# Turning normed tiles with VectorE and scratch memory instead of TensorE, and rebuilding the first weight's sums one group later

## The chip, the cores and the metric

The kernel runs on one core of a Trainium2 chip. The metric is the time of one execution on the device, in microseconds (us), and less is better. The engines are TensorE (PE; its weight loads are listed as PEld), VectorE (DVE), ScalarE (ACT), GpSimd (POOL) and SyncE (SP), which in this kernel issues nearly all DMAs. Each engine runs its own instructions in program order and waits at an instruction until what it needs is ready.

## What is computed

Inputs are q, k and v of shape (8, 8, 576, 64), and two weights of shapes (512, 2048) and (2048, 512), all float32.

```
for each batch, head and chunk of 64 rows:                 # chunk attention
    out = softmax(q_c @ k_c.T / 8) @ v_c
x = out as (8, 576, 512)                                   # heads side by side
u = x + real(fft(fft(x, axis=1), axis=2))                  # Fourier mix
un = (u - mean(u)) / sqrt(var(u) + 1e-6)                   # per row of 512
result = u + relu(un @ w_ch1) @ w_ch2                      # (8, 576, 512)
```

## The kernel before

**Tiles and groups.** The 8 x 576 rows are cut into tiles of 128 rows. Each of the first eight groups holds the four tiles of one batch (two "low", two "high"); the ninth group holds the four tiles of rows left over. For each group the two big products are made: the *up* product (512 to 2048 columns, `w_ch1`) and the *down* product (2048 to 512, `w_ch2`). I write U0 to U8 and D0 to D8 for these phases; they alternate on PE: U0, D0, U1, D1 and so on.

**Two forms of the products.** `up_plain` and `down_plain` use the weights as they are: 64 matmuls of 128x128 by 128x512 a phase. `up_halves` and `down_halves` cut each matrix into halves and make seven half-sized products instead of eight (112 matmuls of 128x128 by 128x256 a phase). They need sums and differences of the weights' quarters. `keep1` (for `w_ch1`) and `keep2` (for `w_ch2`) make these sums once and write the seven operands to scratch memory `s1` and `s2`; from then on `fetch(1)` reads 256 KB slabs of `s1` into ten places in `wa`, and `fetch(2)` reads 1 MB slabs of `s2` into three places in `wb`, over the plain weights. `first_of = {1: 1, 2: 1}` says from which group on the halved forms are used: here both from group 1 on. They need sums of activations too: `combined(g, q_)` (line 860, four VectorE operations) makes them from the turned tiles, for one low and one high tile; `q_` is 0 or 1.

**Turning.** The up product wants the normed rows with the 512 columns on the partitions. `normed(g, s)` (line 830) makes a normed tile `un`; `turned(g, s)` (line 848) transposes it by four 128x128 PE transposes (`turn`, line 329/333) into PSUM, and copies it to `unT` with ACT (line 858) or DVE (line 856).

**Order of the work.** All order is written by hand. `mlp(g)` yields after each step: 16 steps `t` in an up phase and in `down_plain`, 14 steps (`k` = 0 to 13; product `o = k // 2`, low or high tiles `r = k % 2`) in `down_halves`. After each step the launching loop (lines 1213 to 1248) issues a share of the next batch's attention and Fourier work, the rounding of weight pieces at the start, and the steps of `conv1` (`keep1`) and `conv2` (`keep2`). In `down_halves(g)` the next group's tiles are normed at k = 3, 5, 7, 9, turned in the middle of the matmuls of k = 5, 7, 9, 11 (line 1088), and combined at k = 9 and 11 (line 1116). Finished output tiles are stored at k = 10 to 13 by `store` (line 871): a low tile by one 256 KB DMA (line 876), a high tile by two of 128 KB (line 885). Slabs are fetched at the end of odd k (line 1131, issue at line 933).

**The step in question at the start.** `conv1` runs in D0 from t = 23 on, three steps of VectorE work at a time, and from t = 29 the first ten slabs of `s1` are fetched. `conv2` runs on VectorE in U1, four steps at a time, while U1 already uses slabs of `s1`.

Of the kernel before, what the change touches and what calls it, by code (L numbers as in the profile page):

```python
# [8 lines left out]
FP32 = mybir.dt.float32  # L9
# [7 lines left out]
def kernel(  # L17
# [32 lines left out]
    nc = tc.nc  # L50
    B, H, S, D = q.shape
    DM = H * D
# [7 lines left out]
    KD = DM // 128  # L60
# [39 lines left out]
    UP = (1, 0, 2, 3, 4, 6, 5)  # L100
    s1 = dram.tile([HF // 2, NO, 128, 2 * 2 * 128], FP32, name="s1")
    s2 = dram.tile([NO, 128, HF * HM], FP32, name="s2")
    NS1, NS2, Z1, Z2 = 10, 3, 2 * 2 * 128, HF * HM
    slab1 = [wa[:, i * Z1:(i + 1) * Z1].rearrange("p (k r f) -> p k r f", r=2, k=2) for i in range(NS1)]
    slab2 = [wb[:, i * Z2:(i + 1) * Z2].rearrange("p (m e) -> p m e", m=HF) for i in range(NS2)]
# [742 lines left out]
    def turned(g, s):  # L848
# [8 lines left out]
        else:  # L857
            nc.scalar.copy(unT[:, :, s * 128:(s + 1) * 128], pt)

    def combined(g, q_):  # L860

        unT = unTs[g]
        cl, ch = slice(q_ * 128, (q_ + 1) * 128), slice(256 + q_ * 128, 256 + (q_ + 1) * 128)
        b11, b12, b21, b22 = unT[:, 0:2, cl], unT[:, 0:2, ch], unT[:, 2:4, cl], unT[:, 2:4, ch]
        t1, t2, t4 = (tt[:, o, :, cl] for o in range(3))
        nc.vector.tensor_tensor(out=t1, in0=b12, in1=b11, op=ALU.subtract)
        nc.vector.tensor_tensor(out=t2, in0=b22, in1=t1, op=ALU.subtract)
        nc.vector.tensor_tensor(out=b12, in0=b22, in1=b12, op=ALU.subtract)
        nc.vector.tensor_tensor(out=t4, in0=b21, in1=t2, op=ALU.subtract)
# [18 lines left out]
    def keep1(i):  # L888

        f, kk = divmod(i, 2)  # L890
        lo, hi = slice(f * 512, (f + 1) * 512), slice(DFF // 2 + f * 512, DFF // 2 + (f + 1) * 512)
        a11, a12, a21, a22 = w1[:, kk, lo], w1[:, 2 + kk, lo], w1[:, kk, hi], w1[:, 2 + kk, hi]
        late = [xall[:, r, 0:DM] for r in (NR + 2, NR + 3, 2 * G + 2, 2 * G + 3)]
        o1, o2, o3, o4 = late if i % 2 else (yall[:, j] for j in range(4))
        for out_, in0, in1, op in (
            (o1, a21, a22, ALU.add), (o2, o1, a11, ALU.subtract),
            (o3, a11, a21, ALU.subtract), (o4, a12, o2, ALU.subtract),
        ):
            nc.vector.tensor_tensor(out=out_, in0=in0, in1=in1, op=op)
            yield  # L900
        to = s1.rearrange("a o p (k x) -> p a o k x", k=2)[:, 2 * f:2 * f + 2]
        for o, a in enumerate((a11, o2, o1, o3, a12, o4, a22)):
            nc.sync.dma_start(out=to[:, :, o, kk], in_=a.rearrange("p (a x) -> p a x", a=2))
        yield

    def keep2(i):

        m = 2 * i
        b11, b12 = w2[:, m:m + 2, 0:HM], w2[:, m:m + 2, HM:DM]
        b21, b22 = w2[:, HF + m:HF + m + 2, 0:HM], w2[:, HF + m:HF + m + 2, HM:DM]  # L910
        to = xall[:, 0:4, 0:DM] if i % 2 else yall
        o1, o2, o3, o4 = (to[:, j].rearrange("p (m e) -> p m e", m=2) for j in range(4))
        for out_, in0, in1, op in (
            (o1, b12, b11, ALU.subtract), (o2, b22, o1, ALU.subtract),
            (o3, b22, b12, ALU.subtract), (o4, b21, o2, ALU.subtract),
        ):
            nc.vector.tensor_tensor(out=out_, in0=in0, in1=in1, op=op)
            yield
        to = s2.rearrange("o p (m e) -> o p m e", m=HF)
        for o, a in enumerate((b11, o2, o1, o3, b21, b22, o4)):  # L920
            nc.sync.dma_start(out=to[o, :, m:m + 2], in_=a)
        yield

    first_of = {1: 1, 2: 1}
    n_slab = {1: 0, 2: 0}

    def fetch(which):
# [140 lines left out]
    def down_halves(g, h1):  # L1068
        pas, pbs = {}, {}
        for o in range(NO):  # L1070
            w = slab2[((g - first_of[2]) * NO + o) % NS2]
            for r in range(2):
                cl, ch = slice(r * 128, (r + 1) * 128), slice(256 + r * 128, 256 + (r + 1) * 128)
                low, high = groups[g][r], groups[g][2 + r]
                olow, ohigh = os_[:, 2 * r], os_[:, 2 * r + 1]
                a, b = tmp[:, r, 0], tmp[:, r, 1]
                if o == 0:
                    pas[r] = ps_f.tile([128, 2, 256], FP32, tag="ff", name="pa")
                if o == 2:
                    pbs[r] = ps_f.tile([128, 2, 256], FP32, tag="ff", name="pb")  # L1080
                dst = (pas, pas, pbs, pbs, pas, pbs, pbs)[o][r][:, (0, 1, 0, 1, 0, 0, 1)[o]]
                lhs = (
                    h1[:, 0:HF, cl], ys[:, :, cl], xs[:, :, cl], h1[:, 0:HF, ch],
                    h1[:, HF:KF, cl], ys[:, :, cl], h1[:, HF:KF, ch],
                )[o]
                k = 2 * o + r
                for m in range(HF):
                    if m == HF // 2 and g + 1 < NG and k in range(5, 5 + 2 * G, 2):
                        turned(g + 1, (k - 5) // 2)
                    nc.tensor.matmul(  # L1090
                        out=dst, lhsT=lhs[:, m], rhs=w[:, m],
                        start=(o in (0, 2) and m == 0), stop=(m == HF - 1), skip_group_check=True,
                    )
                if o == 0:
                    nc.scalar.copy(a, dst)
                elif o == 1:
                    nc.vector.tensor_tensor(out=b, in0=dst, in1=a, op=ALU.add)
                elif o == 2:
                    nc.vector.tensor_tensor(out=a, in0=dst, in1=b, op=ALU.add)
                elif o == 3:  # L1100
                    nc.vector.tensor_tensor(out=ohigh[:, HM:DM], in0=dst, in1=ohigh[:, HM:DM], op=ALU.add)
                    nc.gpsimd.tensor_tensor(out=olow[:, HM:DM], in0=b, in1=natural(low)[:, HM:DM], op=ALU.add)
                    nc.gpsimd.tensor_tensor(out=ohigh[:, 0:HM], in0=b, in1=natural(high)[:, 0:HM], op=ALU.add)
                elif o == 4:
                    nc.vector.tensor_tensor(out=olow[:, 0:HM], in0=dst, in1=natural(low)[:, 0:HM], op=ALU.add)
                elif o == 5:
                    nc.vector.tensor_tensor(out=olow[:, HM:DM], in0=dst, in1=olow[:, HM:DM], op=ALU.add)
                    store(low, olow)
                else:
                    nc.vector.tensor_tensor(out=ohigh[:, 0:HM], in0=dst, in1=ohigh[:, 0:HM], op=ALU.add)  # L1110
                    store(high, ohigh)
                if g + 1 < NG:
                    for j in range(G):
                        if k == 3 + 2 * j:
                            normed(g + 1, j)
                        if k == 5 + 2 * j and j >= 2:
                            combined(g + 1, j - 2)
                if r == 1:
                    if o == 1:
                        for j in range(0, HF, 2):  # L1120
                            two = ys[:, j:j + 2]
                            nc.gpsimd.tensor_tensor(
                                out=two, in0=h1[:, HF + j:HF + j + 2, lo], in1=two, op=ALU.subtract
                            )
                    if o == 2:
                        for i in range(2):
                            nc.gpsimd.tensor_tensor(
                                out=os_[:, 2 * i + 1, HM:DM], in0=tmp[:, i, 0],
                                in1=natural(groups[g][2 + i])[:, HM:DM], op=ALU.add,
                            )  # L1130
                    fetch(2)
                yield
# [7 lines left out]
    with tc.manual_schedule():  # L1140
# [59 lines left out]
        for g in range(NG):  # L1200
            begin.append(begin[-1] + (KF if g < first_of[1] else 2 * HF) + (KF if g < first_of[2] else 2 * NO))
        ready_at = [begin[g] + (2 * KF - 7 if g < first_of[2] else 2 * HF + 4) for g in range(NG)]
        conv2 = iter([step for i in (2, 3, 0, 1) for step in [keep2(i)]])
        conv1 = iter([step for i in range(4) for step in [keep1(i)]])

        def chain(gens):
# [6 lines left out]
        for g in range(NG):  # L1213
            for _ in mlp(g):
# [15 lines left out]
                    if t <= 2 or t < KF and t % 4 == 0 or t >= KF + 3:  # L1230
                        round_next()

                if n_w > len(pieces) and KF + 7 <= t < begin[1] - 3:
                    for _ in range(3):
                        next(conv1, None)
                if t == begin[1] - 3:
                    for _ in conv1:
                        pass
                    for _ in range(NS1):
                        fetch(1)  # L1240
                if begin[1] <= t:
                    for _ in range(4):
                        next(conv2, None)
                if t == begin[1] + KF // 2 + 2:
                    for _ in conv2:
                        pass
                    for _ in range(NS2):
                        fetch(2)


# [47 lines left out]
```

## Time and profile before

| what | value |
|---|---|
| median of 3 runs | 1115.32 us (1114.74 to 1116.82) |
| the profiled execution | 1116.82 us |
| its span, first to last instruction | 1115.0 us, 1.8 us less than its time |
| PE busy | 1069.9 us, 96% of the span |
| DVE, ACT, POOL busy | 601.9, 304.7, 259.4 us |
| DMA, queue of SP | 149652 packets, 197.54 MB, 60.2% of 16 engines |

Phases on PE, by the first matmul of each:

| phase | from | to | length | its own matmuls |
|---|---|---|---|---|
| D0 | 115.53 | 193.96 | 78.43 | 59.22 (plain, 128x512) |
| U1 | 193.96 | 278.52 | 84.56 | 55.2 (halved) |
| D1 | 278.52 | 340.87 | 62.35 | 50.8 |
| U2 | 340.87 | 399.76 | 58.89 | 50.2 |
| D2 | 399.76 | 456.63 | 56.87 | 50.4 |
| D3, D4, D5 | | | 61.52, 56.87, 61.52 | 50.5 each |
| D6 | 861.20 | 914.71 | 53.51 | 49.8 |
| D7 | 963.06 | 1013.16 | 50.10 | 49.2 |
| U8 | 1013.16 | 1061.51 | 48.35 | 48.35 |
| D8 | 1061.51 | 1110.02 | 48.51 | 48.5 |

How to read it: each matmul of float32 stands as two records. A phase's length less its own matmuls is other PE work (attention, Fourier, turning) and idle time. D8 has no next group to turn, and U8 and D8 have nothing beside their products.

### The profile page before, as it was taken

What the parts mean: (1) busy time and instruction counts of PE and PEld (TensorE: products, weight loads), DVE (VectorE), ACT (ScalarE), POOL (GpSimd) and SP (SyncE); (2) the same over time, 40 slices, a digit from 0 to 9 for tenths busy, and PEclk for the clock granted to TensorE, in tenths of its full rate; (3) what the DMA queues carried; (4) which work ended last, traced back from release to release, by engine and by line L of the source; (5) the groups of instructions that cost most, each with busy time, mean ns of one, the idle gap of its engine ahead of it and who ended that gap; (6) DMA issues with size and microseconds to landing.
All of it is one profiled execution on the core that took longest, in us unless ns stands there. A gap on an engine that the chain in (4) does not pass through costs nothing.

```text
span 1115.0 us, 19182 instructions
## 1 busy us (share of the span) xinstructions
PE 1069.9 (96%) x7114; PEld 869.0 (78%) x7114; DVE 601.9 (54%) x1322; ACT 304.7 (27%) x746; POOL 259.4 (23%) x387
## 2 busy tenths in 40 slices
PE   8999999488999999999999999999999999999998
PEld 6645444366888888888888888888888888888887
DVE  4899988465355645573556356644554434323521
ACT  4787453022112231232122211322133102201210
POOL 4201000005311523051405140334033401130130
PEclk9999999789999999999999999999999999999999
DMA  8778548798756845785467547773754346446332
GB/s 165 227 209 192 145 147 258 223 308 242 221 163 196 215 135 187 212 219 157 162 189 203 176 152 203 190 210 130 205 193 114 114 156 198 138 151 198 85 114 76
DMA packets 152005, 200.11 MB, mean 179 GB/s; under 512 B 66574, under 2 KB 104462, under 8 KB 144744
## 3 DMA queue, kind: packets, MB, share of 16 engines
q1 hardware_dynamic: 149652, 197.54, 60.2%
q8 instruction: 57, 0.93, 0.4%
q0 software_dynamic: 512, 0.68, 0.3%
q10 hardware_dynamic: 1748, 0.66, 0.2%
q14 instruction: 36, 0.29, 0.1%
HBM read 174.56 MB, written 24.12 MB: 178 GB/s over the span
## 4 chain that ended last, share of the span: by engine, by line
PE 84%; DMA 5%; DVE 5%; ACT 3%; SPq 2%; issue 1%; POOL 1%; DVEq 0%; ACTq 0%; POOLq 0%
PE pb L1090 20%; PE pa L1041 19%; PE pa L1090 15%; PE pb L1041 14%; PE pt L333 3%; PE dn L995 3%; PE up L954 2%; PE mix L700 2%; PE more_z L652 2%; DMA wa<-s 2%; PE sc L384 1%; PE xp L432 1%; PE z L652 1%; DMA xall<-in_moe_w_ch_dram 1%; DMA k<-in_k_dram 1%
## 5 line engine op out<-in xcount | busy, mean ns | idle before, releaser
L1041 PE MATMUL pa<-unT,wa 128*128 128x256 f32 x768 | 184.0, 383 | 3.3 <-DVE h L1057 2.7
L1041 PEld LDWEIGHTS pa<-unT,wa 128*128 128x128 f32 x768 | 145.6, 191 | 24.2 <-DVE h L1057 3.5
L1041 PE MATMUL pb<-wa 128*128 128x256 f32 x512 | 124.7, 387 | 5.1 <-DMA wa<-s 3.3
L942 POOL TENSOR_TENSOR h<-h 128x256 f32<-128x256 f32 x64 | 55.7, 874 | 317.3 <-PE pb L1041 150.5
L1090 PE MATMUL pa<-wb,h 128*128 128x256 f32 x512 | 115.6, 380 | 0.0
L1090 PE MATMUL pb<-wb,h 128*128 128x256 f32 x512 | 114.9, 379 | 0.0
L1041 PEld LDWEIGHTS pb<-wa 128*128 128x128 f32 x512 | 97.8, 193 | 20.4 <-issue 3.7
L1090 PEld LDWEIGHTS pa<-wb,h 128*128 128x128 f32 x512 | 96.1, 190 | 13.0
L1090 PEld LDWEIGHTS pb<-wb,h 128*128 128x128 f32 x512 | 96.3, 190 | 12.6
L1047 DVE TENSOR_TENSOR wa<-pb,wa 128x256 f32<-128x256 f32 x64 | 27.0, 425 | 69.3 <-ACT wa L1046 69.1
L1041 PE MATMUL pa<-wa 128*128 128x256 f32 x256 | 61.3, 382 | 1.0 <-DMA wa<-s 1.0
L1046 ACT COPY wa<-pa 128x256 f32<-128x256 f32 x64 | 23.8, 373 | 137.2 <-PE pa L1041 130.6
L1041 PE MATMUL pb<-unT,wa 128*128 128x256 f32 x256 | 60.6, 379 | 0.1
L995 PE MATMUL dn<-wb,h 128*128 128x512 f32 x128 | 59.2, 612 | 1.2 <-ACT h L965 1.2
L1090 PE MATMUL pb<-wb,yall 128*128 128x256 f32 x256 | 58.2, 381 | 0.0
L1090 PE MATMUL pa<-wb,yall 128*128 128x256 f32 x256 | 57.9, 380 | 0.0
L1061 ACT ACTIVATE h<-h 128x512 f32<-128x512 f32 x64 | 39.7, 628 | 66.4 <-DVE h L1060 66.2
L1090 PE MATMUL pb<-wb 128*128 128x256 f32 x256 | 57.7, 379 | 0.0
L1055 ACT ACTIVATE h<-pa 128x256 f32<-128x256 f32 x64 | 24.6, 384 | 112.5 <-PE pa L1041 112.3
L1041 PEld LDWEIGHTS pb<-unT,wa 128*128 128x128 f32 x256 | 48.6, 190 | 7.1 <-DVE wa L1049 0.5
L1041 PEld LDWEIGHTS pa<-wa 128*128 128x128 f32 x256 | 47.9, 190 | 7.8 <-issue 1.1
L1090 PEld LDWEIGHTS pa<-wb,yall 128*128 128x128 f32 x256 | 47.7, 190 | 6.4
(247 smaller groups left out, 1633.0 us busy)
## 6 DMA issues: line engine op xcount, KB each, us to landing
wa<-s SPq DMA_DIRECT2D x224, 256.0 KB
wb<-s SPq DMA_DIRECT2D x56, 1024.0 KB
xall<-in_moe_w_ch_dram SPq DMA_DIRECT2D x22, 512.0 KB
q<-in_q_dram SPq DMA_DIRECT2D x96, 112.0 KB
k<-in_k_dram SPq DMA_DIRECT2D x96, 112.0 KB
v<-in_v_dram SPq DMA_DIRECT2D x124, 64.0 KB
yall<-in_moe_w_ch_dram SPq DMA_DIRECT2D x10, 512.0 KB
s<-yall SPq DMA_DIRECT2D x16, 256.0 KB
```

The costliest lines, as they stand in the source:

```text
L333: nc.tensor.transpose(pt[:, j, :], src(j), ident)
L652: nc.tensor.matmul(out=out_, lhsT=lhsT[p], rhs=tk[p, i, T // 2 if T != 5 else 0, cols], start=start, stop=stop, skip_group_check=True,)
L700: nc.tensor.matmul(out=mix[:, cols], lhsT=zt[:, T], rhs=tab, start=(T == 0), stop=(T == 3), skip_group_check=True,)
L942: nc.gpsimd.tensor_tensor(out=h1[:, m, hi], in0=h1[:, m, lo], in1=h1[:, m, hi], op=ALU.subtract)
L954: nc.tensor.matmul(out=up, lhsT=w1[:, kk, m * 128:(m + 1) * 128], rhs=unT[:, kk], start=(kk == 0), stop=(kk == KD - 1), skip_group_check=True,
L995: nc.tensor.matmul(out=dn, lhsT=h1[:, m, s * 128:(s + 1) * 128], rhs=w2[:, m, :], start=(m == 0), stop=(m == KF - 1),)
L1041: nc.tensor.matmul(out=dst, lhsT=w[:, kk, r], rhs=rhs[o][:, kk], start=(o in (0, 1) and kk == 0), stop=(kk == 1), skip_group_check=True,)
L1046: nc.scalar.copy(a, dst)
L1047: nc.vector.tensor_tensor(out=b, in0=pbs[r][:, 0], in1=a, op=ALU.add)
L1055: nc.scalar.activation(out=h1[:, m, lo], in_=dst, func=ACTF.Relu)
L1061: nc.scalar.activation(out=h1[:, HF + m], in_=h1[:, HF + m], func=ACTF.Relu)
L1090: nc.tensor.matmul(out=dst, lhsT=lhs[:, m], rhs=w[:, m], start=(o in (0, 2) and m == 0), stop=(m == HF - 1), skip_group_check=True,)
```

## The change

Three edits are made at once.

1. **Turning.** In `down_halves` the PE transposes go. After `normed(g+1, j)` at k = 3 + 2j, `flipped` transposes the tile's 32x32 blocks on VectorE into `blocks`; at k = 4 + 2j `sent` writes the blocks to scratch memory by four DMAs in pieces of 128 bytes, such that memory holds the turned tile; at k = 5 + 2j `fetched` reads 256 KB back into `unT`. `combined` moves to k = 11 (q_ = 0) and 12 (q_ = 1). This holds for groups 2 to 8; group 1 is turned by PE in `down_plain(0)` as before.
2. **First use of the halves.** `first_of[1]` goes from 1 to 2: U1 uses `up_plain`, and group 1 is not combined.
3. **Sums of weights.** `conv2` is now in D0 (VectorE, three steps at a time from t = 23), in the order 0, 1, 2, 3 and with `xall[2G:2G+4]` in place of `xall[0:4]`; `conv1` is now in U1 on GpSimd, three steps at a time in its first eight steps, with `os_` in place of rows of `xall`. The first slabs of `s2` are fetched in the middle of U1, those of `s1` at its end.

```diff
+    un_d = [dram.tile([128, KD, G * 128], FP32, name=f"un_d{i}") for i in range(2)]
...
+    def flipped(g, s):
+        if s >= len(groups[g]):
+            return
+        un = uns.pop((g, s))
+        t = three_p.tile([128, KF, 32], FP32, tag="o", name="blocks")
+        nc.vector.transpose(out=t, in_=un.rearrange("p (b f) -> p b f", f=32))
+        blocks[g, s] = t
+
+    def sent(g, s):
+        if s >= len(groups[g]):
+            return
+        t = blocks.pop((g, s))
+        to = un_d[g % 2].rearrange("(a f) k t -> f k a t", a=4)
+        for i in range(4):
+            nc.sync.dma_start(
+                out=to[:, :, :, s * 128 + 32 * i:s * 128 + 32 * (i + 1)],
+                in_=t[32 * i:32 * (i + 1)].rearrange("f (k a) t -> f k a t", a=4),
+            )
+
+    def fetched(g, s):
+        if s >= len(groups[g]):
+            return
+        if s == 0:
+            unTs[g] = one_p.tile([128, KD, G * 128], FP32, tag="unT", name="unT")
+        cols = slice(s * 128, (s + 1) * 128)
+        nc.sync.dma_start(out=unTs[g][:, :, cols], in_=un_d[g % 2][:, :, cols])
...
-        late = [xall[:, r, 0:DM] for r in (NR + 2, NR + 3, 2 * G + 2, 2 * G + 3)]
-        o1, o2, o3, o4 = late if i % 2 else (yall[:, j] for j in range(4))
+        o1, o2, o3, o4 = ((os_ if i % 2 else yall)[:, j] for j in range(4))
...
-            nc.vector.tensor_tensor(out=out_, in0=in0, in1=in1, op=op)
+            nc.gpsimd.tensor_tensor(out=out_, in0=in0, in1=in1, op=op)
...
-        to = xall[:, 0:4, 0:DM] if i % 2 else yall
+        to = xall[:, 2 * G:2 * G + 4, 0:DM] if i % 2 else yall
...
-    first_of = {1: 1, 2: 1}
+    first_of = {1: 2, 2: 1}
...
-                    if m == HF // 2 and g + 1 < NG and k in range(5, 5 + 2 * G, 2):
-                        turned(g + 1, (k - 5) // 2)
...
-                        if k == 5 + 2 * j and j >= 2:
+                            flipped(g + 1, j)
+                        if k == 4 + 2 * j:
+                            sent(g + 1, j)
+                        if k == 5 + 2 * j:
+                            fetched(g + 1, j)
+                        if k == 6 + 2 * j + (j == 2) and j >= 2:
                             combined(g + 1, j - 2)
...
-        conv2 = iter([step for i in (2, 3, 0, 1) for step in [keep2(i)]])
+        conv2 = iter([step for i in range(HF // 2) for step in [keep2(i)]])
...
-                if n_w > len(pieces) and KF + 7 <= t < begin[1] - 3:
+                if n_w > len(pieces) and t >= KF + 7:
+                    for _ in range(3):
+                        next(conv2, None)
+                if t == begin[1] - 1:
+                    for _ in conv2:
+                        pass
+                if begin[1] <= t < begin[1] + KF // 2:
                     for _ in range(3):
                         next(conv1, None)
-                if t == begin[1] - 3:
-                    for _ in conv1:
-                        pass
+                if t == begin[1] + KF // 2:
+                    for _ in range(NS2):
+                        fetch(2)
+                if t == begin[1] + KF:
                     for _ in range(NS1):
                         fetch(1)
-                if begin[1] <= t:
-                    for _ in range(4):
-                        next(conv2, None)
-                if t == begin[1] + KF // 2 + 2:
-                    for _ in conv2:
-                        pass
-                    for _ in range(NS2):
-                        fetch(2)
```

More of the change, by code (lines that the diff above doesn't have):

```diff
@@ L858, in turned @@
             nc.scalar.copy(unT[:, :, s * 128:(s + 1) * 128], pt)
+    blocks = {}
+    def flipped(g, s):
[22 more added lines that the diff above has]
+        nc.sync.dma_start(out=unTs[g][:, :, cols], in_=un_d[g % 2][:, :, cols])
     def combined(g, q_):
```

## The prediction

> **What bounds the kernel now.** I read the page's busy rows first, then the windows of single phases, the waits inside U1, and SP's own timeline at a phase boundary.
>
> ```profile
> span 1115.0 us, 19182 instructions
> ...
> PE 1069.9 (96%) x7114; PEld 869.0 (78%) x7114; DVE 601.9 (54%) x1322; ACT 304.7 (27%) x746; POOL 259.4 (23%) x387
> ...
> PEclk9999999789999999999999999999999999999999
> ```
>
> PE is busy for 96% of the span, so a change pays only by taking work off PE or by closing one of its few gaps. PE's largest hole lies in slices 8 and 9, which are U1, where PEclk also drops. The windows give, for U1, U2, D7 and D8: length, busy time (and instructions) of PE, PEld, DVE, ACT, POOL, then the granted clock, the DMA share and GB/s.
>
> ```profile
> 193.96:278.52 84.56, 60.67 (x464) 50.44 (x465) 45.88 (x102) 17.11 (x38) 17.38 (x33) 0.86 0.88 259
> 340.87:399.76 58.89, 58.49 (x415) 49.12 (x409) 35.07 (x79) 17.18 (x42) 19.95 (x34) 1.00 0.74 207
> 963.06:1013.16 50.10, 50.10 (x241) 44.12 (x240) 13.73 (x30) 2.62 (x6) 11.43 (x12) 1.00 0.42 145
> 1061.51:1110.02 48.51, 48.51 (x225) 42.37 (x223) 7.14 (x16) 1.45 (x4) 11.04 (x12) 1.00 0.30 104
> ```
>
> U2, D7 and D8 are full of PE work; U1 has 84.56 - 60.67 = 23.9 us without any, and its clock is 0.86 where the others have 1.00. The waits in U1 (who waited <- for whom: us, times, longest) say why:
>
> ```profile
> PE pt L333 <- ACT ex L410: 16.9, 1, 16.9
> ...
> DVE yall L917 <- DMA s<-yall: 15.7, 1, 15.7
> ```
>
> VectorE stands 15.7 us in `conv2`, whose buffer is still being written to scratch memory; the attention behind it is late, and PE with it.
>
> **Part 1: PE without the turning.** In D7 the turning is this, with the copy after it:
>
> ```profile
> 1004.09 0.60 PE L333 MATMUL pt<-ident,un 128*128 128x128 f32 x4
> 1004.73 0.69 DVE L856 COPY unT<-pt 128x512 f32<-128x512 f32 x1 [1.67 <-PE pt L333]
> ```
>
> D7 and D8 have the same product and differ by the turning of four tiles: 50.10 - 48.51 = 1.59 us a group, less than the 4 x 0.60 of busy time because PE's records overlap. Seven groups (2 to 8) give -7 x 1.59 = -11.1 (to -16.8 by busy time). The copy of a tile goes too (0.69 us on VectorE or 0.58 on ACT).
>
> What VectorE gets for it stands in the trace as the same form:
>
> ```profile
> L352 DVE STREAM_TRANSPOSE kT<-k 128x512 f32<-128x512 f32 x27 | 30.0, 1111 | 8.4 <-DMA k<-in_k_dram 8.2
> ```
>
> So 28 tiles x 1.11 = 31 us of VectorE, less about 14 copies x 0.69 = 10. VectorE is busy 13.73 of 50.10 us in D7 and 35 of 59 in U2, so I cost this at nothing; if that cover went, (31 - 10) / 7 = 3 us a group would show.
>
> **Part 1: the path of the last tile.** This decides the sum. Before, a tile was turned within 2 us; now it goes out (4 DMAs, 512 pieces of 128 bytes each) and back (256 KB), and PE's next up phase cannot start before `combined` has had tile 3. Its writes are issued at k = 10, on SP directly after the store of the first low output tile (line 876). SP's timeline at the end of D7 shows that store at 1003.09, the last PE work of D7 ending at 1013.16, 10.07 later:
>
> ```profile
> 1003.09 0.56 SPq L876 DMA_DIRECT2D out_dram<-wb  x1
> 1006.98 1.13 SPq L885 DMA_DIRECT2D out_dram<-wb  x2
> 1008.20 0.54 SPq L933 DMA_DIRECT2D wb<-s  x1
> 1010.36 0.55 SPq L876 DMA_DIRECT2D out_dram<-wb  x1
> ```
>
> No view prints when a DMA landed; I counted it from the semaphore updates in the trace. The L876 store lands 7.80 to 7.91 us after its issue in each of D1 to D7 and its updates come from only 2 of 16 engines, while the two halves of a high tile (L885), issued 3.9 us after it, land only 0.3 to 0.4 us after it (1010.89, then 1011.22). So what is issued behind this store has its share on the two busy engines wait, and the new writes stand just there. Steps from that store's issue: it lands at 7.85; the writes' share on those engines, 4 x 512 / 16 = 128 pieces, follows; then about 0.3 for the reading DMA, which waits for the writes; then 2.5 to 2.6 for 256 KB (a slab of `wa` lands in 2.5 at best). A piece of 128 bytes takes 11 to 12 ns on an engine in this trace (224 packets, other DMAs), one of 256 bytes 18 to 21, one of 1024 bytes 46 to 49. Those are not scattered writes. I take 16 ns, between the first two: 128 x 0.016 = 2.05, so the tile is back X = 7.85 + 2.05 + 0.3 + 2.6 = 12.8 us after the store. Bounds: 11 ns (nearest row; X = 12.2) and 49 ns (an eight times larger piece; X = 17.0).
>
> The Trainium skill, "DMA: Bandwidth & Descriptors", section "Specifications", speaks against these writes: pieces under 512 bytes do not reach line rate and are paid as read-modify-write. The small packets above do not show that, and no run here has scattered 128-byte writes; paid like whole 512-byte pieces (about 30 ns, between the rows above), an estimate by that page's rule, they would add 1.8 us to each of seven groups, and the sum would be some 12 us higher.
>
> What waits: a second `combined` is 4 operations of 0.42 on VectorE, some 1.75; PE's first matmuls of the up phase use the first sums 0.95 after tile 3 is there. Before, the up phase began 11.70 us after the store in D1 to D5 and 10.07 in D6 and D7; without the last turning (0.44 in the chain) that is 11.26 and 9.63. In D1, D3 and D5 an attention product stands ahead on PE at 10.7, and the VectorE transposes that it needs are now behind all of the second `combined` (1.75 + 1.1, less what overlaps: 2.75). Stalls:
> - D1, D3, D5: 12.8 + 2.75 - 10.7 = 4.85 each, 14.6
> - D2, D4: 12.8 + 0.95 - 11.26 = 2.5 each, 5.0
> - D6, D7: 12.8 + 0.95 - 9.63 = 4.1 each, 8.2
>
> Together 27.8; with X = 12.2 it is 23.6, with X = 17.0 it is 57. Slabs and stores queued on SP behind the waiting read of 256 KB come some 3 us later; slabs are issued about a phase before use, so I cost that at nothing, or up to 1 us a group (7) without that cover.
>
> **The clock after a stall.** In U1, after PE idle of some 3.5 us or more, the granted clock stands at 0.50 for pieces of 3.41 us (231.21 to 234.62, 258.52 to 261.93): each costs 1.7 us. About half of the five long stalls should get one: +4 (0 to 8.5). The Trainium skill, "TensorE: Matmul & The Clock Gate", Part 1, has the clock halve after an idle window of this length, in agreement.
>
> **Part 2 and 3: U1 and D0.** U1 becomes plain. D0's plain product gives its size:
>
> ```profile
> L995 PE MATMUL dn<-wb,h 128*128 128x512 f32 x128 | 59.2, 612 | 1.2 <-ACT h L965 1.2
> ```
>
> 59.2 us of matmuls, 4 more than the 55.2 that the halved form takes in U1. The other PE work of U1 is 60.67 - 55.2 = 5.5 in the window's busy time and 7.2 as a sum of its groups, so U1 has at least 64.7 to do; I take 59.2 + 7.2 = 66.4. What is late next is SP: 76 DMAs are issued from 190 on at about 0.69 us each (SP's rate in U1), with the writes of `s1`, the stores and the shift of batch 2 among them, so the last q and k tiles of that batch are turned near 241 and 248, by my count some 6 us after PE could use them. So U1 is 66.4 + 6 = 72, and 84.56 - 72 = -12.5 (-18 without that wait, -4 if the attention is as late by 8 us more). The sums of `w_ch1` move to GpSimd: 16 operations of 1.39 (line 1122 has the form: 1391 ns) are 22 us in U1, where POOL is busy 17 of 84; nothing on PE waits for them before U2. `conv2` in D0 takes the VectorE place that `conv1` had (the same 16 operations). The `combined` of group 1, which stood ahead of the last output rows of D0, goes: -1.4.
>
> **Sum.** -11.1 (turning) - 12.5 (U1) - 1.4 (D0) + 27.8 (starts of seven up phases) + 4 (clock) = +6.8. The profiled execution took 1116.82 (span 1115.0 and 1.8 around it), which is 1.5 above the median 1115.32; against the median the forecast is **1122 us**. Measurements of this kernel can tell about 0.2%, 2.2 us, from no change.
>
> **The rivals.**
> - *The forecast*: waits at the starts of U2 to U8 eat both gains. For it: a store that lands late in every group, directly ahead of the writes. Bounds: 1122 - 4 - 4 = 1114 (11 ns, no clock pieces), 1108 if U1 also gains 18; upwards 9 (26 ns a piece: 10 ns x 128 x 7), 4.5 (all clock pieces), 8.5 (U1 gains only 4) and 2 (slabs), 1146. Chance **0.55**, of which 0.05 is faster and 0.07 within 0.2%.
> - *The exchange is hidden*, the side not slower: pieces go round the two busy engines, or the queue takes DMAs side by side, so X is near 9 (1.4 for the writes beside the store, and issue, wait, and 2.6). Stalls are then about 3 and the clock keeps 1.00: 1115.3 - 25 + 3 = 1093. It wins once X is below some 9.6, the point from which U7 and U8 start on time. Against it: L885 landing just after L876 in all pairs I looked at. Chance **0.22**.
> - *Small writes are dear*: at 49 ns X = 17, stalls 57, clock +8.5: 1115.3 - 25 + 57 + 8.5 = 1156, and SP's queue falls back in every group. For it: no scattered write of 128 bytes is in this trace to say otherwise. Chance **0.13**.
> - *U1 keeps its hole*: the attention in U1 is as late as before, now behind SP's queue; nothing is gained there, so 1122 + 12 = 1134. Chance **0.10**, of which 0.03 falls within 0.2% with an exchange half hidden.
> - That the turning does not leave PE: excluded, since in `down_halves` nothing else calls it.
>
> **Numbers.** Slower by over 0.2%: (0.55 - 0.05 - 0.07) + 0.13 + 0.07 = 0.63. Faster: 0.22 + 0.05 = 0.27. Same: 0.07 + 0.03 = 0.10. The range is 1093 to 1146: it leaves out half of the hidden case (0.11) and most of the dear one (0.09), together 0.2. The forecast's own range is 1108 to 1146.
>
> **What would show it.** In the profile after: no PE work on line 333 past D0, D7 near 48.5; PE waiting at the first matmuls of U2 to U8 for VectorE's `combined`, and that for a DMA into `unT`, some 2.5 us in U3 and U5, 4 to 5 in U2, U4, U6, U7 and U8; PEclk dips there; U1 near 72 with PE waiting for q or k. If U7 and U8 start as before, the store does not hold the writes and the forecast is wrong by 25 us; if D0 to U1 grows, the SP queue there was mis-sized.

## The result, and the profile after

| | before | after |
|---|---|---|
| median of the runs beside each other | 1115.03 us (1113.09 to 1116.82) | 1139.68 us (1139.17 to 1141.52) |
| ratio, 95% interval | | 1.0224 (1.0204 to 1.0245) |
| span of the profiled execution | 1115.0 us | 1137.6 us |
| PE idle after 115 us (start of D0) | 31.0 us | 47.4 us |
| PE's time lost to a clock of 0.50 | 6.5 us | 19.3 us |

The change makes the kernel slower by 2.24% (24.65 us between the medians); 1122 was forecast. The two lower rows are counted from the trace's records of the profiled execution: the time up to PE's last instruction in which no PE instruction ran, and half of PE's busy time that lay in stretches granted 0.50.

The changed kernel's page, its busy row and its clock row:

```profile
PE 1075.8 (95%) x6906; PEld 848.9 (75%) x6906; DVE 591.8 (52%) x1272; ACT 292.6 (26%) x716; POOL 280.1 (25%) x403
...
PEclk9999999999989998999899998999899989998999
```

The one dip of before (U1) is gone. In its place stand seven, one for each group turned by scratch memory. PE's busy time is larger although it has 208 instructions less: matmuls in stretches granted 0.50 last longer and count as busy (19.3 us of PE's time against 6.5, the last row of the table).

The windows of U1, U2, D7, U8 and D8 of the changed kernel, with the columns of the prediction's windows:

```profile
191.82:253.99 62.17, 61.65 (x369) 29.31 (x368) 19.00 (x42) 12.44 (x22) 27.28 (x36) 1.00 0.73 222
321.99:381.18 59.19, 59.19 (x413) 50.27 (x409) 34.83 (x77) 17.41 (x42) 19.91 (x34) 0.97 0.74 205
978.79:1032.92 54.13, 48.51 (x226) 42.38 (x224) 14.65 (x31) 1.44 (x4) 11.43 (x12) 0.99 0.56 165
1032.92:1084.11 51.19, 51.19 (x225) 44.63 (x226) 22.38 (x54) 13.72 (x31) 5.38 (x6) 0.95 0.43 133
1084.11:1132.61 48.50, 48.50 (x225) 42.37 (x223) 7.15 (x16) 1.44 (x4) 11.04 (x12) 1.00 0.31 104
```

U1 is 62.17 us where it was 84.56, and full of work. D7's PE work is 48.51, exactly D8's, so the turning is off PE as meant; but D7 lasts 54.13, with 5.6 idle at its end, and U8 after it has a mean clock of 0.95 and takes 51.19 instead of 48.35. Up to the start of D1 the changed kernel gains 24.5 us (253.99 against 278.52); from there to the end of U8 it loses 47.1 (830.12 against 782.99).

PE's two largest waits in the whole changed kernel (who waits <- for whom: us, times, longest):

```profile
PE pb L1070 <- DVE wa L897: 23.4, 4, 6.5
PE sc L385 <- DVE kT L353: 20.1, 3, 7.3
```

The four are the starts of U3, U5, U7 and U8, which wait for `combined` (line 897). The three are attention products just ahead of U2, U4 and U6, whose VectorE transposes (line 353) stand behind `combined`. Together 43.5 us. The chain of waits from D7 into U8 tells what `combined` waited for (start, us, what):

```profile
1017.05 0.44 DVE wb L1134
...
1017.50 0.58 SPq L906
...
1018.13 0.60 SPq L877
...
1018.77 2.99 SPq L877
...
1021.80 2.42 SPq L877
...
1024.26 4.52 DMA un_d<-blocks
...
1028.92 3.03 DMA unT<-un_d
...
1031.98 0.44 DVE wa L896
...
1032.44 0.43 DVE wa L897
...
1032.92 1.22 PE pb L1070 x2
```

The store of the low tile (now line 906) is issued, then the four writes, of which the last lands at 1028.78; then the read of 256 KB, then `combined`, then PE. The second and third writes take SP 2.99 and 2.42 us to issue. By the semaphore updates the store lands at 1027.25, 9.75 after its issue, and the last write 1.53 behind it. The slab of `wb` that is issued 1.16 us ahead of the store (1016.34) lands at 1022.08, so it stands ahead of both.

### The profile page after: what moved, and what is told of

Its sections match the earlier page's. It is cut to its first block, busy times and chain, and to the rows that moved or that the text cites. A ratio compares the mean times of both kernels' runs of the same rounds, so it can differ in the third digit from the quotient of the medians.

```text
span 1137.6 us, 18806 instructions
## 1 busy us (share of the span) xinstructions
PE 1075.8 (95%) x6906; PEld 848.9 (75%) x6906; DVE 591.8 (52%) x1272; ACT 292.6 (26%) x716; POOL 280.1 (25%) x403
## 4 chain that ended last, share of the span: by engine, by line
PE 75%; DMA 10%; SPq 5%; DVE 5%; ACT 2%; issue 1%; POOL 1%; DVEq 0%; ACTq 0%; POOLq 0%
PE pa L1070 17%; PE pb L1070 14%; PE pa L1117 13%; PE pb L1117 11%; PE up L1003 4%; DMA un_d<-blocks 4%; PE up L983 3%; SPq L877 3%; PE dn L1024 3%; DMA wb<-s 3%; DMA unT<-un_d 2%; PE mix L701 2%; PE more_z L653 2%; PE sc L385 1%; PE z L653 1%; PE pt L334 1%
## 5 line engine op out<-in xcount | busy, mean ns | idle before, releaser
L1070 PE MATMUL pa<-unT,wa 128*128 128x256 f32 x672 | 163.1, 387 | 0.0
L1070 PEld LDWEIGHTS pa<-unT,wa 128*128 128x128 f32 x672 | 130.4, 196 | 19.0
L1070 PE MATMUL pb<-wa 128*128 128x256 f32 x448 | 119.0, 413 | 23.4 <-DVE wa L897 23.4
L1070 PEld LDWEIGHTS pb<-wa 128*128 128x128 f32 x448 | 91.7, 208 | 38.6 <-DVE wa L897 24.4
L1003 PE MATMUL up<-unT,wa 128*128 128x512 f32 x128 | 56.8, 595 | 0.0
L718 POOL TENSOR_TENSOR xall<-y,xall 128x513 f32<-128x513 f32 x14 | 24.0, 1711 | 124.3 <-DVE y L712 114.3
L1070 PE MATMUL pa<-wa 128*128 128x256 f32 x224 | 53.5, 382 | 0.0
L1117 PEld LDWEIGHTS pb<-wb,yall 128*128 128x128 f32 x256 | 48.2, 190 | 6.7
L1070 PE MATMUL pb<-unT,wa 128*128 128x256 f32 x224 | 52.9, 379 | 0.0
L1117 PEld LDWEIGHTS pb<-wb 128*128 128x128 f32 x256 | 48.2, 190 | 6.3
```

The costliest lines, as they stand in the source:

```text
L718: eng.tensor_tensor(out=x[:, 0:w], in0=y[:, 0:w], in1=x[:, 0:w], op=ALU.add)
L1003: nc.tensor.matmul(out=up, lhsT=w1[:, kk, m * 128:(m + 1) * 128], rhs=unT[:, kk], start=(kk == 0), stop=(kk == KD - 1),)
L1070: nc.tensor.matmul(out=dst, lhsT=w[:, kk, r], rhs=rhs[o][:, kk], start=(o in (0, 1) and kk == 0), stop=(kk == 1), skip_group_check=True,)
L1117: nc.tensor.matmul(out=dst, lhsT=lhs[:, m], rhs=w[:, m], start=(o in (0, 2) and m == 0), stop=(m == HF - 1), skip_group_check=True,)
```

## The experiments

All medians are in us; the ratio is to the kernel before, run beside it on the same chip (medians 1112.3 to 1112.7). "Idle" and "clock" are the two lower rows of the table above, each from one profiled execution, which in e2, e7 and e9 was the slowest of its runs. "New order" is the changed kernel with edits 2 and 3 alone. e2, e3, e4, e7, e11 and e13 scatter more than the others, by 6 to 14 us (e4 from 1114.3 to 1124.5), so their ratios carry the weight.

| run | what | median | ratio, 95% interval | idle | clock |
|---|---|---|---|---|---|
| e1 | new order, turned by PE | 1088.65 | 0.9789 (0.9762 to 0.9815) | 5.2 | 0 |
| e2 | before + turning by scratch memory | 1162.73 | 1.0451 (1.0411 to 1.0491) | 76.4 | 24.2 |
| e3 | after, low store on 16 engines | 1103.28 | 0.9937 (0.9909 to 0.9966) | 21.4 | 8.6 |
| e4 | after, stores behind the last read | 1120.95 | 1.0063 (1.0040 to 1.0087) | 36.7 | 8.1 |
| e7 | e3 and e4 together | 1095.86 | 0.9828 (0.9787 to 0.9870) | 18.5 | 5.0 |
| e11 | after, writes issued by ACT | 1143.55 | 1.0271 (1.0239 to 1.0303) | 52.6 | 14.0 |
| e5 | new order, three tiles by scratch memory | 1091.11 | 0.9811 (0.9797 to 0.9826) | 11.3 | 3.1 |
| e12 | e5, writes issued by ACT | 1100.87 | 0.9887 (0.9855 to 0.9918) | 17.9 | 7.5 |
| e9 | e1 + block transposes | 1092.73 | 0.9822 (0.9796 to 0.9848) | 9.3 | 1.7 |
| e10 | e9 + one plain write a tile | 1094.08 | 0.9830 (0.9806 to 0.9855) | 7.4 | 1.7 |
| e14 | e9 + four plain writes a tile | 1101.38 | 0.9889 (0.9867 to 0.9912) | 10.7 | 3.4 |
| e6 | e9 + the four writes of edit 1 | 1104.58 | 0.9939 (0.9919 to 0.9958) | 17.1 | 1.7 |
| e8 | e1, `w_ch1` sums on VectorE | 1092.22 | 0.9821 (0.9806 to 0.9835) | 8.0 | 0 |
| e13 | e1, `w_ch2` sums in U1 | 1111.04 | 0.9981 (0.9965 to 0.9997) | 19.7 | 5.7 |

### e1 and e2: the two halves of the change

e1 puts `turned` back into the matmul loop of `down_halves` and the two `combined` back to k = 9 and 11. e2 is the diff of edit 1 on the kernel before.

> The changed kernel with edits 2 and 3 only: group 1 plain, sums of w_ch2 in D0 and of w_ch1 in U1 on GpSimd; all tiles turned by PE as before. Theory (the order of the sums closes the hole in U1, 22.4 us in the trace after, and the exchange costs what D1 to U8 lost): 1115 - 25 = 1090, within 3, no idle time of PE above 2 us after U1. Rival (part of the gain before D1 came from the exchange's lighter PE, or the hole comes back later): 1097 to 1110.

> The kernel before with edit 1 only: tiles of groups 2 to 8 turned by VectorE and scratch memory, the sums' order as before. Theory: the hole of U1 stays and D1 to U8 grow by 47 us as in the trace after: 1162, within 4, seven stalls of 4.8 to 7.3 us of PE. Rival (the stalls of after come from the later sums or slabs of edits 2 and 3): below 1145.

The theory held in both. The new order alone is worth -24.0 us (1088.65 against 1112.63) and the exchange alone costs +50.1; on top of the new order the exchange costs 1139.68 - 1088.65 = +51.0 (48.6 if each is taken against its own kernel before). So the halves add up to within some 2 us and can be explained apart. e1's page shows a PE without a hole:

```profile
PE 1068.5 (98%) x7018; PEld 847.4 (78%) x7018; DVE 577.1 (53%) x1258; ACT 299.2 (28%) x730; POOL 280.6 (26%) x403
...
PEclk9999999999999999999999999999999999999999
```

e1 is also the fastest version found: 2.1% faster than the kernel before.

### e3, e4, e7: the store ahead of the writes

e3 and e4 as diffs of the changed kernel; e7 has both.

```diff
 # e3
-            nc.sync.dma_start(out=to[:, ::-1], in_=o)
+            for i in range(2):
+                nc.sync.dma_start(out=to[i], in_=o[i * CH:(i + 1) * CH])
 # e4
-                    store(low, olow)
+                    late.append((low, olow))
...
+                if k == 11:
+                    for n, o_ in late:
+                        store(n, o_)
```

> The changed kernel, with the store of a low tile cut into two DMAs of 64 rows, whose rows go out in unreversed order (this leaves out the reversal of the rows), so that it is spread over 16 engines instead of 2. Theory (the last tile's writes are held by the two engines of that store): the store lands some 5 us earlier, the tile comes back some 5 us earlier, stalls shrink from 43 us in all to under 15 and most pieces at clock 0.50 go: 1090 to 1100. Rival (many small writes, their issue and the way back are the cost themselves): above 1125.

> The changed kernel, with both output tiles of k = 10 and 11 stored on SP only after the last tile's writes and its read have been issued; every DMA keeps its form. Theory: the writes stand behind a slab of wb only, the tile is back some 5 us earlier, stalls under 15 us in all: 1085 to 1100. Rival (small writes themselves, or the slab of wb ahead of them, set the time): above 1120.

> The changed kernel with both edits: output tiles of k = 10 and 11 stored after the last read is issued, and a low tile stored by two DMAs over 16 engines with its rows unreversed (this leaves out the reversal of the rows). Theory (the two-engine store holds whatever stands behind it: the writes in the changed kernel, the slabs and loads when it is moved): neither is held now, 1080 to 1092. Rival (moving stores late costs by itself, or the small writes do): above 1100.

e3 takes back 36 of the 51 us by the medians, 32 of 48 by the ratios: less than expected (1090 to 1100) and far from the rival. Its store in D7 still lands 5.4 us after its issue; the 1 MB slab of `wb`, issued 1.1 us before it, lands only 0.35 ahead of it. Writes and read follow, and the tile is back 10.7 us after the store's issue instead of 14.45. PE's boundary waits are 18.6 us in all.

e4 failed as a remedy, in a way that tells something. Its time, 1120.95, lies at the edge of the rival's range (above 1120), but its waits are not the rival's:

```profile
PE pa L1070 <- DVE h L1086: 9.3, 3, 3.3
PE pb L1070 <- DMA wa<-s: 9.0, 6, 2.7
PE pb L1070 <- DVE wa L897: 6.0, 4, 2.2
```

The waits for `combined` fell from 23.4 to 6.0, as the theory says. But PE now waits inside the up phases, 9.0 us of it directly for slabs of `wa`. SP's own timeline shows the two low stores close behind each other:

```profile
1013.66 0.56 SPq L888 DMA_DIRECT2D unT<-un_d  x1
1014.26 0.58 SPq L906 DMA_DIRECT2D out_dram<-wb  x1
1014.95 1.18 SPq L915 DMA_DIRECT2D out_dram<-wb  x2
1016.17 1.63 SPq L962 DMA_DIRECT2D wb<-s  x1
1017.85 0.80 SPq L906 DMA_DIRECT2D out_dram<-wb  x1
```

By the semaphore updates the first lands 8.1 us after its issue, the second 13.6, and the slabs behind them 9.8 to 11.9 (the three of `wa` 11.2 to 11.9, where slabs of `wa` have a median of 4.0 in the changed kernel). So what stands behind the two-engine store on SP lands late: the writes in one order, the slabs in the other. e7, with the store on 16 engines and late, is at 1095.86: between theory (up to 1092) and rival (from 1100), still above e1. From the issue of the last tile's first write to the landing of its read, the mean of the seven groups is 13.1 us in the changed kernel, 9.0 in e3, 9.1 in e4 and 9.2 in e7. With the store spread over 16 engines, issued later, or both, this way is some 4 us shorter, and 9 us remain; how much of them is due to the slab of `wb` ahead of the writes was not tried apart. What a perfectly placed exchange could gain, the 11 us of turning, no version got.

### e11: the writes on another queue

```diff
-            nc.sync.dma_start(
+            nc.scalar.dma_start(
                 out=to[:, :, :, s * 128 + 32 * i:s * 128 + 32 * (i + 1)],
```

> The changed kernel with the four writes of a tile issued by ACT instead of SP; the read stays on SP. Theory (the writes stand behind the two-engine store because they follow it in SP's queue): they land some 5 us earlier, the tile is back some 4 us earlier, and PE's stalls fall from 43 us to 10 to 20: 1100 to 1115. Rival (the two engines themselves are busy with the store, whichever queue the writes come from): 1133 to 1142.

The time lies just past the rival's range (1143.55; the range ended at 1142), but not by the rival's mechanism: the writes hardly meet the store. In D3 ACT and SP issue as follows:

```profile
542.54 2.94 ACTq L877 DMA_DIRECT2D un_d<-blocks  x4
...
552.91 0.62 SPq L906 DMA_DIRECT2D out_dram<-wb  x1
...
554.93 0.74 SPq L888 DMA_DIRECT2D unT<-un_d  x1
```

By the semaphore updates all four writes have landed at 549.90, 11.5 us ahead of the store (561.39). From ACT the last write is issued ahead of the store in every group, by 3.5 to 9.4 us in D1 to D5 and by 0.6 and 0.25 in D6 and D7, and in D1 to D6 it lands 4.2 to 11.6 us ahead of it. So far the theory is right. But the read that brings the tile back is still on SP and is now what stands behind the store: in D3 it is issued 5.0 us after the writes have landed and takes 8.71 us, where the changed kernel's reads of the last tile take 3.03 to 3.65. In all seven groups it lands 1.4 to 3.4 us behind the store. From the end of its block transpose the last tile needs 19.3 us on average to be back, where the changed kernel needs 18.5: moving the writes alone only changed which part of its way was held. In D7 alone the writes were late too:

```profile
1016.59 2.85 ACTq L877 DMA_DIRECT2D un_d<-blocks  x4
...
1019.04 0.57 SPq L906 DMA_DIRECT2D out_dram<-wb  x1
...
1029.25 0.57 SPq L888 DMA_DIRECT2D unT<-un_d  x1
```

All four writes (the third and fourth at 1018.17 and 1018.79) are issued before the store. The first two land at once, but the third lands at 1026.24, just after a slab of `wb` that SP issued at 1018.41, and the fourth at 1029.19, 10.4 us after its issue; the store takes 12.3 us instead of 9.75. That would fit two transfers sharing the two engines, but it is one group of seven. Whether a transfer issued behind the store, such as the read, would go round it from another queue was not tried.

### e5, e12: only the last tile by PE

> The changed kernel with the fourth tile of each group turned by PE again (in the middle of k = 11, both combined at k = 11); the first three go through scratch memory. Theory (only the last tile's way back is on the path, the others have 3 us and more to spare): three quarters of the 11 us of turning are saved on the version with the new order alone, 1088.65 - 8 = 1080, within 4, no stall over 2 us at the starts of U2 to U8. Rival (the DMAs of the other tiles delay slabs and loads on SP's queue, or tile 2 is late as well): 1095 or more.

> The fourth tile turned by PE, the first three through scratch memory with their writes issued by ACT. Theory (what kept this from beating the new order alone was SP's queue): 1080 to 1087. Rival (the writes cost wherever they are issued, or ACT's work is now late): 1089 to 1095.

In e5, `flipped`, `sent` and `fetched` are called for j < 3 only, and `turned(g + 1, 3)` stands in the matmul loop of k = 11. The boundary waits are gone, and D7 is 48.79 us where e1 has 50.10. Still the total is 1091.11, no better than e1: the theory (1080) fell, and the rival's mechanism held with less of it (it said 1095 or more). PE now waits up to 2.2 us inside U2 to U5, for slabs and for VectorE. With the writes on ACT (e12) it is 9.8 us worse, with 8.4 us of waits for slabs of `wa`; the theory that SP's queue alone was the trouble fell.

### e6, e9, e10, e14: the exchange as a pure load

These add parts of edit 1 to e1 whose result nothing reads, while PE does the turning. e9 has the block transposes alone; e10 and e14 write the blocks to a plain buffer in rows of 2 KB, by one DMA and by four; e6 writes as edit 1 does.

```diff
 # e10
+        nc.sync.dma_start(out=flat_d[g % 2, s], in_=t.rearrange("p k f -> p (k f)"))
 # e14
+        for i in range(4):
+            p = slice(32 * i, 32 * (i + 1))
+            nc.sync.dma_start(out=flat_d[g % 2, s, p], in_=t[p].rearrange("p k f -> p (k f)"))
```

> The version with the new order alone (all tiles turned by PE), plus the block transposes on VectorE and the writes to scratch memory of edit 1, which nothing reads: 31 us more of VectorE and 112 DMAs of 64 KB in pieces of 128 bytes as pure load. Theory (the exchange costs by its wait, not by its load): 1088.65 to 1093. Rival (112 DMAs on SP and the pieces of 128 bytes crowd out slabs, loads and stores, or VectorE's added work is on the path): 1100 or more.

> The version with the new order alone, plus only the block transposes on VectorE (28 x 1.1 us), whose result nothing uses; no writes. Theory A (the 16 us that the writes cost as pure load are SP's and the DMA queues'): 1088 to 1092. Theory B (they are VectorE's added work): 1100 to 1106.

> The version with the new order alone, plus the block transposes and one plain write of 256 KB per tile in rows of 2 KB, instead of four DMAs in pieces of 128 bytes; nothing reads it. Theory A1 (what costs is the number of DMAs and pieces): 1089 to 1095. Theory A2 (what costs is that any write at these places waits on SP's queue and stands ahead of slabs, loads and stores): 1100 to 1105, as with four writes.

> The version with the new order alone, plus the block transposes and four plain writes of 64 KB per tile in rows of 2 KB, which nothing reads: the number of DMAs of edit 1, without its small pieces. Theory A (the number of DMAs on SP's queue costs the 10 us between one plain write, 1094.1, and four writes in pieces of 128 bytes, 1104.6): 1101 to 1106. Theory B (the pieces of 128 bytes cost it): 1092 to 1096.

My theory of e6 fell: writes that nobody waits for cost 15.9 us. The steps are +4.1 (block transposes), +1.3 (one write), +7.3 (four DMAs instead of one), +3.2 (pieces of 128 bytes). By the ratios they are +3.7, +0.9, +6.6 and +5.6. The first two are within the intervals; in each of the last two steps the intervals of the two runs just miss each other, so these steps are likely but not sharp. The third is the number of DMAs, as theory A of e14 said. PE in e6 waits 5.6 us for slabs of `wa` and 6.3 for VectorE work (line 1078).

### e8, e13: what closed the hole in U1

e8 puts `nc.vector` back into `keep1`. e13 takes `conv2` out of D0 and runs it in U1, three steps at a time, beside `conv1` on GpSimd. In e13 the temporaries of `conv1` (`os_`) lie over part of `w_ch2` that is not yet summed, so its sums of `w_ch2` are partly other numbers; the operations and their sizes are the same.

> The version with the new order alone, but the sums of w_ch1 in U1 on VectorE as before instead of GpSimd. Theory (the hole of U1 is VectorE waiting, in order, for buffers still being written to scratch memory, with the attention queued behind it): the hole comes back in part, PE idle 5 to 17 us in U1, 1095 to 1107. Rival (the plain product in U1, which needs no slab, closes the hole whichever engine sums): 1087 to 1091.

> The version with the new order alone, but the sums of w_ch2 on VectorE in U1 as before (buffers yall and the rows of batch 0), with U1 still plain and the sums of w_ch1 on GpSimd beside them. Theory (the hole of U1 was VectorE waiting in U1 for a buffer whose write to scratch memory is late on SP): the hole comes back, PE idle 8 us or more in U1 and D1, 1098 to 1115. Rival (the plain form of U1, which reads no slabs, closes the hole wherever the sums are made): 1086 to 1093.

In e8 the theory fell: the same sums on VectorE cost 3.6 us, with one stall of 2.4, and the intervals of e1 and e8 overlap (1092.22 lies just above the rival's range). It is not GpSimd that closes the hole. In e13 the hole is back in a plain U1, which refutes the rival. Its waits from 185 to 330 us, and then PE's in the whole kernel:

```profile
POOL yall L928 <- DMA s<-yall: 27.7, 2, 15.2
...
DVE xall L946 <- POOL wb L928: 16.0, 1, 16.0
```

```profile
PE sc L385 <- DVE rd L446: 8.7, 1, 8.7
PE sc L385 <- DVE kT L353: 7.9, 3, 6.0
```

VectorE stands 16.0 us in the sums (line 946) for a GpSimd sum (line 928), which itself waits for buffers still being written to scratch memory, and PE idles 14.7 us in two pieces for attention work queued behind it on VectorE. The dependence is not quite the one of before (GpSimd stands between), but it is the same place: sums with late buffers, on the engine that the attention needs, in the phase that has most DMAs. What the plain form of U1 gives by itself was not tried apart.

## Why the prediction was wrong, point by point

The sign, the mechanism and the places of the waits were right; the size was wrong. Three terms were mis-sized: U1 in one direction, the waits and the clock in the other. That the time lies inside the range is partly luck: with only the 12.5 us that U1 was to gain, instead of 22.4, it would have been near 1150, above the range's 1146.

- **Turning off PE, -11.1**: right. D7 without its stall is 48.51, as D8; over D1 to U8 PE's busy time, less what the clock cost, is 11.8 us smaller. The block transpose took 0.71 us, not the 1.11 of the row that I had as its like:

```profile
L868 DVE STREAM_TRANSPOSE blocks<-un 128x512 f32<-128x512 f32 x28 | 19.9, 711 | 1.0
```

- **D0, -1.4**: about right, -1.9.
- **U1, -12.5**: measured -22.4. Two steps failed. The first is "what is late next is SP", 6 us of waiting: SP's pace was about as I said, and the last k tiles of that batch landed at 250.79, but PE did not want them in U1 (its next product with k is at 283.11, in D1). PE is idle for 0.5 us in the changed kernel's U1. I had counted when the loads land and only guessed when PE would use them. The second is the work itself, 66.4 us: it was 61.65. U1's 128 matmuls took 595 ns each on average (56.8 us), where D0's had taken 612, some of them at a clock of 0.50; and the other PE work took 4.9 us, where I had taken the 7.2 of a sum of groups.
- **Waits at the starts, +27.8**: measured 43.5. The tile's way, from the store's issue in D1 to D7, was on average 13.76 us (12.70 to 15.23), where I had 12.8. The parts: the store 8.02 to 9.75 (I had 7.85), the writes 1.51 to 1.63 behind it (2.05), the read's issue 0.05 to 0.14, but 1.60 and 1.12 in D2 and D4 (0.3), the read 3.03 to 3.65 (2.6). So 128 pieces of 128 bytes cost 12 ns each by the landings (13 by the median of the packets' own records), near the nearest row and not the dearer one that I took. These parts make 6.7 of the missing 15.7 us. The other 9.0 come from a step that I had put at nothing, "slabs and stores queued on SP behind the waiting read come some 3 us later; I cost that at nothing" (its range had 2 us of the 7 named there): one of those stores is the very store that holds the writes. In D3 the changed kernel's timeline has

```profile
547.38 0.42 DVE L1134 TENSOR_TENSOR wb<-pb,wb 128x256 f32<-128x256 f32 x1 [0.71 <-PE pb L1117]
547.80 2.76 SPq L219 DMA_DIRECT2D v<-in_v_dram  x4
550.66 0.61 SPq L906 DMA_DIRECT2D out_dram<-wb  x1
```

  The output tile is ready at 547.80 and its store is issued at 550.66, behind the read of the third tile, a slab and four v loads. In D1 to D5 the store is issued 1.15 to 2.86 us after its tile is ready, where in the kernel before it was 0.03. So PE was through 8.04 to 9.75 us after the store in D1 to D5, where I had 10.7 and 11.26; in D6 and D7, where SP has no loads and the store is issued at once (0.03), 9.80 against 9.63.
- **The clock, +4**: measured +17.85 over the seven stalls. I had given half of five stalls one piece of 3.41 us. By the clock records all seven got 0.50, five for 6.83 us and two for 10.24, and 4.2 to 6.1 us of PE's work fell into each. The stalls were 4.8 to 7.3 us long. The two pieces of 3.41 that I read in U1 followed stalls of 2.42 and 3.28 us, not "some 3.5 us or more", so less idle time than the window that the prediction cited was enough here; and I passed over the third piece of that trace, 17.07 us (five times 3.41) with the stall of 16.9, which showed that a longer stall gets more than one piece.

The sum by phases: -24.5 up to D1 (forecast -13.9) and +47.1 from D1 to U8 (forecast 27.8 + 4 - 11.1 = +20.7), together +22.6, which is the difference of the spans. By the trace's records the second part is all accounted for: PE's idle time went from 2.4 to 43.5 (+41.1), the clock cost 17.85, and PE's work shrank by 11.8.

- **The rivals.** "The exchange is hidden" was excluded by the store, as I had weighed it; its point, X below 9.6 in D6 and D7, was not reached even in e3 (10.5 and 10.7 there; 8.8 to 11.6 in the others). "Small writes are dear" is wrong for the piece (12 ns) and half right in another sense: four DMAs a tile and their pieces cost 16 us with their transposes as a load (e6), which my sum had as nothing to 7. In the changed kernel this load shows in no wait of its own: the 43.5 us that PE is idle from D1 to U8 are the seven stalls.

The Trainium skill's page "DMA: Bandwidth & Descriptors", section "Why a DMA increments its semaphore by 16 and not by 1", says that a DMA runs on as many engines, up to 16, as divide the slowest dimension (other than 1) of both of its access patterns. In the store's destination that dimension is 2, and by the updates it runs on 2 engines; the rows unreversed in e3, with a slowest dimension of 64, ran on 16. The runs agree with the page. The same page's row on pieces under 512 bytes (section "Specifications") led the prediction to an estimate of about 30 ns a piece, the cost of a whole one of 512 bytes. In the changed kernel's trace packets of 128 bytes took 13 ns and packets of 512 bytes 27 (medians), so no run here shows that cost.

## What to carry to other kernels

When an engine's work is replaced by a round trip through memory, price the last round trip before a barrier by its place in the issuing queue: what stands ahead of it, on how many DMA engines that runs, and which waiting DMA delays the issue of what stands ahead. A store that runs on two engines did no harm here until something with a deadline stood behind it; moving one part of that (the writes) to another queue did not help, because the next part (the read) was still behind the store. And try the parts of a combined change alone: here one half was worth -24 us and the other some +50.

## What the runs showed that I had not expected

- A stall of 4.8 to 7.3 us was followed not by one but by two or three pieces of 3.41 us at clock 0.50 (6.83 and 10.24 us), beginning before PE took up its work.
- VectorE's block transpose of 128x512 float32 took 0.71 us for `blocks<-un`, whose two sides are laid out densely, and 1.11 for `kT<-k`, whose sides are strided; the records show the same shape. That the layout is the reason was not tried.
- Writes on ACT's queue landed 4.2 to 11.6 us ahead of the two-engine store on SP's in six groups, and still the tile was not back earlier; in the seventh group one that was issued 0.25 us ahead of the store landed 10.4 us after its issue, and the store slowed to 12.3.
- 84 more DMAs (four instead of one for 28 tiles, same bytes) cost about 7 us in a kernel whose DMA engines are busy for some 60% of the time.
